# Products whose result is never read, in TensorE's queue during the first batch's attention

## The chip, the core and the metric

The kernel runs on one core of one Trainium2 chip. The metric is the device time of one execution in microseconds (us), as the median of several runs. Work is spread over five engines with a queue each: TensorE (PE, products and transposes), VectorE (DVE), ScalarE (ACT), GpSimd (POOL) and SyncE (SP), which here only issues transfers. Each engine takes the instructions of its queue in order; semaphores make one engine wait for another or for a transfer.

## What is computed

Three stages on 4 sequences of 576 positions, 512 wide, in float32:

```python
q_d, k_d, v_d = (t.reshape(B, H, Sd, 4, D).mean(axis=3) for t in (q, k, v))
out_d = sm_attn(q_d, k_d, v_d)                 # attention over 144 means
scores = np.where(abs(i - j) < 4, scale * q @ k.T, -1e9)
x = np.repeat(out_d, 4, axis=2) + softmax(scores) @ v

xk = mu_k * x + (1 - mu_k) * x_prev            # x_prev: the position before
xr = mu_r * x + (1 - mu_r) * x_prev
x = sigmoid(xr @ w_r) * (np.maximum(xk @ w_k, 0) ** 2 @ w_v)

h = np.maximum(x @ w_in, 0)
out = (h * sigmoid(conv3(h)) @ w_out)          # conv3: three taps along the sequence
```

There are 8 heads of 64, w_k and w_in are 512 x 1024, w_v and w_out 1024 x 512, w_r 512 x 512.

## The kernel before

The attention of a batch is done by groups of four heads (two groups, `gp` 0 and 1), and in the first batch each group also in two parts of the sequence: blocks 0 to `half`, then the rest. One part of one group is a chain of steps over four engines, each named by its tag:

- `ld`: SP loads kq (keys and queries), vw (the windows of v) and vp (v for the means). For the first batch, DVE folds vp to vd (L455, L456) and sums kq to kqd (L476, tag `kd`).
- `s`, local scores: PE adds the mask by products of `ident16` with `mask` (L504) and the scores (L513) in an a2 buffer of PSUM; DVE takes the maximum off (L530, L531), ACT the exponential (L539), DVE sums and normalizes (L542, L484, L485, L548) into probs.
- `ds`, down scores, over the means: PE (L575), DVE maximum (L591, L592), ACT exponential with sums (L598), DVE normalizes (L610) into pd.
- `do`: PE transposes pd (L639), ACT copies that to pdt (L647), PE multiplies by vd (L662), ACT copies to od (L674, L676).
- `lo`: PE transposes probs (L694), ACT copies to pt (L699), PE multiplies by vw (L713), DVE adds od and writes xT (L728).

Then `mix_prep` makes xk from xT: an ACT and a DVE instruction for each of four row blocks (L776, L782). The first half of the first batch goes through `first_mix` in plain float32: for each of eight column blocks `mt` of w_k an up product (L808, mm buffers of PSUM in turn: `mt` 0 in `mm_t[0]`, `mt` 1 in `mm_t[1]`), then relu and square on ACT (L820, L825) or DVE (L827), then the down products with w_v (L836). The second part of the first batch's attention and the first group of the second batch's are woven in between. All later halves go through `mix` (L869, L918) with each number split in two fp32r parts, three products in place of one; then gate, hidden layer and output (L1180, L1221, L1301).

A weight slice of 512 KB is loaded to one of three st_d buffers (L374), cut to a float on ACT and DVE (L379, L380, L361, L364) into one of four st_f buffers (st_f, st_ff), and split into its fp32r parts (L400 or L402, L406). An st_f buffer is free when the product that reads it and the split are done, an st_d buffer when L364 is.

The order isn't that of the code. Every piece of work is a `step` with an engine, an estimated time, the keys that it reads and writes, and at most a due time. `Program.order` computes for each step the latest time at which it should start, from its due time and from those that need it, less a number by tag from the table `EARLY`; then it plays the program through: an engine that is free takes, of the steps that are ready by its own estimates, that with the lowest latest time. That play sets each engine's order for good. A step that needs more estimated time therefore moves others, on all engines and to the end of the program.

Of the kernel before, what the change touches and what calls it, by code (L numbers as in the profile page):

```python
# [61 lines left out]
def windows(S, FAC):  # L62

    BQ = 32
    W = BQ + 2 * (FAC - 1)
    return BQ, W, [min(max(BQ * i - FAC + 1, 0), S - W) for i in range(S // BQ)]


class Program:
# [15 lines left out]
    def step(self, engine, us, f, r=(), w=(), due=None, slack=1.0):  # L85
        n = len(self.steps)
        deps = set()
        for k in r:
            if k in self.writer:
                deps.add(self.writer[k])  # L90
        for k in w:
            deps.update(self.readers.pop(k, ()))
            if k in self.writer:
                deps.add(self.writer[k])
        for k in r:
            self.readers.setdefault(k, set()).add(n)
        for k in w:
            self.writer[k] = n
        deps.discard(n)
        self.steps.append((engine, us, f, due, slack))  # L100
        self.tags.append(self.tag)
        self.deps.append(deps)
        return n
# [95 lines left out]
def dve(n):  # L199
    return 0.13 + 1.1e-3 * n  # L200
# [6 lines left out]
def act(n):  # L207
    return 0.155 + 0.93e-3 * n
# [6 lines left out]
def pe(n):  # L215
    return 6.6e-3 + 0.439e-3 * n
# [3 lines left out]
def tile_local_attention__then__channel_mix__then__conv_glu(  # L220
# [16 lines left out]
    nc = tc.nc  # L237
    B, NP, P, S = kq.shape
# [10 lines left out]
    BQ, W, starts = windows(S, FAC)  # L249
# [13 lines left out]
    prog = Program({"DVE": nc.vector, "POOL": nc.gpsimd, "ACT": nc.scalar})  # L263
    both = ("DVE", "POOL")
    step = prog.step
# [11 lines left out]
    ident16 = const.tile([P, P], BF16, name="ident16")  # L277
# [7 lines left out]
    mask = const.tile([P, 3, W], BF16, name="mask")  # L285
# [17 lines left out]
    def several(pool_, n, shape, dtype, name):  # L303
        return [pool_.tile(shape, dtype, name=f"{name}{i}") for i in range(n)]
# [14 lines left out]
    kqd = several(att, 1, [P, 2, 2 * SD], F32, "kqd") + several(first, 1, [P, 2, 2 * SD], F32, "kqd_f")  # L319
# [14 lines left out]
    mm_t = several(ps, 2, [P, 512], F32, "mm")  # L334
# [6 lines left out]
    def ring(name, tiles, one=0):  # L341

        i = count[name] = count.get(name, -1) + 1
        i %= one or len(tiles)
        return tiles[i], (name, i)
# [40 lines left out]
    def weight(src, hi, lo, r, nr, c0, key, need=(), use=None, c_at=0):  # L386

        prog.tag = key, r // nr, c0
        f, fk = floats(src, r, nr, c0)
        if use is not None:  # L390
            prog.tag = key, "first"
            use(f, fk)
            prog.tag = key, "parts", r // nr, c0
        nc_ = 512 // nr
        at = (slice(None), slice(r, r + nr), slice(c0 - c_at, c0 - c_at + nc_))
        part = (r // nr, c0 // nc_)

        def high(e):
            if e is nc.scalar:
                e.copy(hi()[at], f)  # L400
            else:
                e.tensor_copy(hi()[at], f)  # L402

        step(("ACT", "DVE"), (0.62, 0.43), high, [fk, *need], [(key, "h", *part)])
        step(
            "DVE", 0.69, lambda: nc.vector.tensor_sub(lo()[at], f, hi()[at].bitcast(F32)),  # L406
            [fk, (key, "h", *part), *need], [(key, "l", *part)],
        )
# [5 lines left out]
    def group(b, gp):  # L414
# [3 lines left out]
        g = {"kq": [ring("kq", kq_t, 2 * (b > 0)) for _ in pairs], "kqd": ring("kqd", kqd, int(b > 0)), "vw": ring("vw", vw_t, int(b > 0)),  # L418
             "vd": ring("vd", vd_t, int(b > 0))}
# [260 lines left out]
        def local_out(i0, i1):  # L680
# [24 lines left out]
            for pr, hp in enumerate(pairs):  # L705
# [30 lines left out]
                step("DVE", 0.8, add, [odk], [(pk, 0), (pk, 1)] + ks, slack=SL[i0 > 0])  # L736

        return {"loads": loads, "kqd": pooled_kq, "s": local_scores, "ds": down_scores,
                "do": down_out, "lo": local_out}

    def store_x(b):
        prog.tag = "sx", b
# [9 lines left out]
    PACE = 1.32  # L752

    def due(us, pace=1.0):
        t = clock[0]
        clock[0] += us * pace
        return t

    def mix_prep(b, nh):
        prog.tag = "mp", b, nh  # L760
        c0 = nh * NH
        whole = b == nh == 0
        if not whole:
            xk, key = ring("xk", xk_t)
        fs = []
        for kt in range(KM):
            x = xT[b % 2][:, kt]
            cur, prev = x[:, 1 + c0:1 + c0 + NH], x[:, c0:c0 + NH]
            i = count["t"] = count.get("t", -1) + 1
            t, tk = tmp[:, i % 2], ("tmp", i % 2)  # L770
            n = (2, 3, 6, 7)[kt] if whole else 2 + i % 2
            f, fk = tmp[:, n], ("tmp", n)
            xs = [("xT", b % 2, kt, 0)] + ([("xT", b % 2, kt, half)] if nh else [])
            step(
                "ACT", 0.53,
                lambda t=t, prev=prev, kt=kt: nc.scalar.activation(  # L776
                    t, prev, AF.Copy, scale=mus[:, 1, kt:kt + 1]),
                xs + ["mus"], [tk],
            )
            step(  # L780
                "DVE", dve(NH),
                lambda t=t, f=f, cur=cur, kt=kt: nc.vector.scalar_tensor_tensor(  # L782
                    out=f, in0=cur, scalar=mus[:, 0, kt:kt + 1], in1=t, op0=ALU.mult, op1=ALU.add),
                xs + [tk], [fk],
            )
            if whole:
                fs.append((f, fk))
                continue
            h, lo = xk[:, 0, kt], xk[:, 1, kt]
            step("ACT", act(NH), lambda h=h, f=f: nc.scalar.copy(h, f), [fk], [(key, 0, kt)])  # L790
            step(
                ("DVE",), (dve(NH),), lambda e, h=h, lo=lo, f=f: e.tensor_sub(lo, f, h.bitcast(F32)),
                [fk, (key, 0, kt)], [(key, 1, kt)],
            )
        return (fs,) if whole else (xk, key)

    def first_mix(xs):

        squares = xT[1].rearrange("p a s -> p (a s)")[:, 0:KF * NH].rearrange("p (k s) -> p k s", k=KF)
        over = [("xT", 1, x, c) for x in range(KM) for c in (0, half)]  # L800

        for mt in range(KF):
            pst, pk = ring("mm", mm_t)

            def up(w, wk, mt=mt, pst=pst, pk=pk):
                def f():
                    for kt in range(KM):
                        nc.tensor.matmul(  # L808
                            pst[:, 0:NH], lhsT=w[:, kt], rhs=xs[kt][0], start=(kt == 0), stop=(kt == KM - 1)
                        )  # L810

                us = 4 * KM * pe(NH)
                step("PE", us, f, [wk] + [k for _, k in xs], [pk], due=due(us, PACE))

            weight(w_k, lambda: wk_t[0], lambda: wk_t[1], 0, 4, mt * P, "wk", use=up)
            prog.tag = "up", 0, 0
            r, rk = tmp[:, 4 + mt % 2], ("tmp", 4 + mt % 2)
            step(
                "ACT", act(NH) - 0.03,
                lambda r=r, pst=pst: nc.scalar.activation(r, pst[:, 0:NH], AF.Relu), (), [pk, rk],  # L820
            )

            def square(e, r=r, mt=mt):
                if e is nc.scalar:
                    e.activation(squares[:, mt], r, AF.Square)  # L825
                else:
                    e.tensor_tensor(out=squares[:, mt], in0=r, in1=r, op=ALU.mult)  # L827

            step(("ACT", "DVE"), (act(NH), 0.46), square, [rk], [("sq", mt)])
        for mt in range(KM):  # L830
            pst, pk = ring("mm", mm_t)
            for a in range(0, KF, 4):
                def down(w, wk, a=a, pst=pst, pk=pk):
                    def f():
                        for kt in range(a, a + 4):
                            nc.tensor.matmul(  # L836
                                pst[:, 0:NH], lhsT=w[:, kt - a], rhs=squares[:, kt],
                                start=(kt == 0), stop=(kt == KF - 1),
                            )

                    us = 16 * pe(NH)
                    step(
                        "PE", us, f, [wk] + [("sq", kt) for kt in range(a, a + 4)] + over, [pk], due=due(us, PACE)
                    )

                weight(w_v, lambda: wv_t[0], lambda: wv_t[1], a, 4, mt * P, "wv", use=down)
            prog.tag = "dn", 0, 0
            out_of_mix(mt, pst, pk, 0)
# [93 lines left out]
    g0 = [group(0, gp) for gp in range(NG)]  # L942
# [16 lines left out]
    def attend(gs, i0, i1, later=None):  # L959
        for g in gs:  # L960
            g["kqd"](i0, i1)
            g["s"](i0, i1)
            g["ds"](i0, i1)
        for g in gs:
            g["do"](i0, i1)
            g["lo"](i0, i1)

    attend(g0, 0, half)
    xk = mix_prep(0, 0)
    for gp in range(NG):  # L970
        g0[gp]["loads"](half, NB)
# [432 lines left out]
```

## Time and profile before

| | |
|---|---|
| median of 3 runs | 584.84 us |
| lowest and highest run | 584.05, 585.73 us |
| span of the profiled execution | 584.2 us |
| PE busy | 553.3 us (95%), 5900 products |
| DVE, ACT, POOL busy | 380.5, 329.3, 52.0 us |
| chain of work that ended last | PE 82%, DVE 7%, DMA 5%, ACT 3% |

The span is that of the execution from its first to its last instruction; all times of the trace count from its start. "Idle before" is the time for which an engine stood still ahead of an instruction, and the name behind the arrow what ended it. The granted clock (PEclk) is a share of 2.4 GHz: 1.00 is that level, 0.50 is 1.2 GHz. An instruction's duration on PE reaches to a modelled end, so that those of a row overlap; where the time per instruction matters, it is read from start to start.

### The profile page before, as it was taken

How to read it: one execution, taken by the hardware profiler on the slowest of the kernel's cores; microseconds unless marked ns; L12 is line 12 of the kernel's file. 1: busy time of each engine (PE TensorE's matmuls, PEld its weight loads, DVE VectorE, ACT ScalarE, POOL GpSimd, SP SyncE). 2: the span in 40 equal slices, each digit the busy share in tenths (PEclk: the TensorE clock that was granted, in tenths of full speed). 3: DMA queues.
4: the chain of work that ended last, by engine and by line, in shares of the span. 5: the costliest groups of instructions: out<-in, count | busy, mean ns of one | idle time of the engine just before them, and what ended most of it. 6: DMA issues, size and time to landing. Idle time of an engine off the chain costs nothing.

```text
span 584.2 us, 14308 instructions
## 1 busy us (share of the span) xinstructions
PE 553.3 (95%) x5900; PEld 510.7 (87%) x5900; DVE 380.5 (65%) x795; ACT 329.3 (56%) x779; POOL 52.0 (9%) x133
## 2 busy tenths in 40 slices
PE   4579979899999999999999999999999999999996
PEld 3457758789999999999999999899899898998995
DVE  6787698688534355344925899587586686395580
ACT  2458678576646475455838865455454455363441
POOL 3002021021121312110000000000000000000000
PEclk9999989898999999999999999999999999999999
DMA  9858998869467576712530530310400400100101
GB/s 262 292 191 216 296 293 209 283 181 302 141 136 207 113 220 160 171 51 76 187 116 2 202 110 0 123 42 0 146 18 1 145 19 1 54 2 1 54 2 54
DMA packets 42449, 74.14 MB, mean 127 GB/s; under 512 B 3648, under 2 KB 28736, under 8 KB 41472
## 3 DMA queue, kind: packets, MB, share of 16 engines
q1 hardware_dynamic: 38064, 65.27, 33.7%
q0 software_dynamic: 4320, 7.97, 8.9%
q8 instruction: 46, 0.75, 0.5%
q14 instruction: 19, 0.16, 0.1%
HBM read 59.06 MB, written 14.16 MB: 125 GB/s over the span
## 4 chain that ended last, share of the span: by engine, by line
PE 82%; DVE 7%; DMA 5%; ACT 3%; issue 2%; SPq 1%; ACTq 0%; POOL 0%; DVEq 0%
PE a L1301 17%; PE mm L869 15%; PE mm L918 15%; PE a L1221 8%; PE mm L1221 7%; PE mm L1180 4%; PE a L1180 4%; PE a L713 3%; DMA st_d<-in_moe_w_k 2%; DMA st_d<-in_moe_w_v 2%; PE a L694 2%; PE mm L836 2%; PE mm L808 1%; PE a L513 1%; PE a L639 1%
## 5 line engine op out<-in xcount | busy, mean ns | idle before, releaser
L1301 PE MATMUL a<-wk,wv 128*128 128x512 f32 x432 | 100.9, 390 | 0.0
L918 PE MATMUL mm<-k,wv 128*128 128x288 f32 x672 | 97.4, 301 | 0.2 <-ACT tmp L888 0.2
L1301 PEld LDWEIGHTS a<-wk,wv 128*128 128x128 f32 x432 | 80.9, 188 | 15.8
L869 PE MATMUL mm<-xk,wk 128*128 128x288 f32 x672 | 94.6, 299 | 0.0
L918 PEld LDWEIGHTS mm<-k,wv 128*128 128x128 f32 x672 | 91.9, 191 | 0.8 <-ACT tmp L888 0.5
L869 PEld LDWEIGHTS mm<-xk,wk 128*128 128x128 f32 x672 | 91.1, 191 | 1.1 <-issue 0.5
L1221 PE MATMUL mm<-k,wi 128*128 128x386 f32 x288 | 53.2, 338 | 0.4 <-ACT k L1205 0.3
L1221 PE MATMUL a<-k,wi 128*128 128x386 f32 x288 | 53.1, 338 | 0.0
L906 DVE TENSOR_TENSOR k<-tmp,k 128x288 fp32r<-128x288 f32 x56 | 25.7, 464 | 41.9 <-ACT k L899 41.2
L1221 PEld LDWEIGHTS mm<-k,wi 128*128 128x128 f32 x288 | 50.7, 188 | 1.5 <-ACT k L1205 0.7
L1221 PEld LDWEIGHTS a<-k,wi 128*128 128x128 f32 x288 | 50.8, 188 | 0.2
L728 DVE TENSOR_TENSOR xT<-a,od 128x288 f32<-128x288 f32 (+2 forms) x40 | 13.8, 392 | 37.6 <-PE a L713 37.6
L1276 ACT ACTIVATE tmp<-tmp 128x384 f32<-128x384 f32 x48 | 25.1, 523 | 21.6 <-DVE tmp L1270 21.6
L1266 DVE TENSOR_SCALAR tmp<-h,cw_sb 128x384 f32<-128x384 f32 x48 | 20.0, 417 | 25.6 <-ACT h L1251 12.2
L888 ACT ACTIVATE tmp<-mm 128x288 f32<-128x288 f32 x56 | 23.0, 412 | 22.3 <-PE mm L869 22.1
L1270 DVE SCALAR_TENSOR_TENSOR tmp<-h,cw_sb,tmp 128x384 f32<-128x384 f32 x48 | 29.7, 619 | 2.6
L1267 DVE SCALAR_TENSOR_TENSOR tmp<-h,cw_sb,tmp 128x384 f32<-128x384 f32 x48 | 29.7, 619 | 2.3
L1316 ACT ACTIVATE xT<-a 128x512 f32<-128x512 f32 x18 | 10.3, 597 | 36.2 <-PE a L1301 34.4
L1286 ACT CAST wv<-tmp 128x384 fp32r<-128x384 f32 x48 | 24.1, 511 | 9.3 <-DVE tmp L1279 9.2
L1279 DVE SCALAR_TENSOR_TENSOR tmp<-tmp,h 128x384 f32<-128x384 f32 x48 | 25.9, 553 | 3.0 <-ACT tmp L1276 2.5
L1288 DVE TENSOR_TENSOR wv<-tmp,wv 128x384 fp32r<-128x384 f32 x48 | 25.7, 553 | 2.9 <-ACT wv L1286 2.3
L361 DVE SCALAR_TENSOR_TENSOR st_f<-st_f,st_d 128x512 uint32<-128x512 uint32 x28 | 20.3, 725 | 11.1 <-ACT st_d L380 10.8
(149 smaller groups left out, 889.1 us busy)
## 6 DMA issues: line engine op xcount, KB each, us to landing
kq<-in_kq SPq DMA_DIRECT2D x12, 576.0 KB, 5.0
vw<-in_vw SPq DMA_DIRECT2D x6, 1152.0 KB, 9.5
kqd<-in_kqp POOLq DMA_DIRECT2D x18, 288.0 KB, 5.5
x_d<-xT SPq DMA_DIRECT2D x16, 288.0 KB, 7.0
v_d<-tmp SPq DMA_DIRECT2D x32, 144.0 KB, 4.0
out_dram<-xT SPq DMA_DIRECT2D x18, 256.0 KB, 2.0
st_d<-in_moe_w_k SPq DMA_DIRECT2D x8, 512.0 KB, 4.5
st_d<-in_moe_w_v SPq DMA_DIRECT2D x8, 512.0 KB, 5.4
```

Source lines behind the costliest of these rows:

```text
L869: nc.tensor.matmul(pst[:, 0:NH], lhsT=wk_t[wt][:, kt, mt * P:(mt + 1) * P], rhs=xk[:, xs, kt, :], start=(kt == 0 and g == 0), stop=(kt == ...
L906: ("DVE",), (dve(NH),), lambda e, r=r, kh=kh, kl=kl: e.tensor_sub(kl, r, kh.bitcast(F32)),
L918: nc.tensor.matmul(pst[:, 0:NH], lhsT=wv_t[wt][:, kt, mt * P:(mt + 1) * P], rhs=xs, start=(kt == 0 and g == 0), stop=(kt == KF - 1 and g = ...
L1180: nc.tensor.matmul(pst[:, 0:CW], lhsT=late["wr"][wt][:, kt, mt * P:(mt + 1) * P], rhs=r_t[xs][:, kt, :], start=(kt == 0 and g == 0), stop= ...
L1221: nc.tensor.matmul(pst[:, 0:CW], lhsT=late["wi%d" % (mt * P // HF)][wt][:, kt, mt * P % HF:mt * P % HF + P], rhs=x1s[xs][:, kt, :], start= ...
L1267: nc.vector.scalar_tensor_tensor(out=cv, in0=tap(0), scalar=cw[:, 0, mt:mt + 1], in1=cv, op0=ALU.mult, op1=ALU.add)
L1270: nc.vector.scalar_tensor_tensor(out=cv, in0=tap(2), scalar=cw[:, 2, mt:mt + 1], in1=cv, op0=ALU.mult, op1=ALU.add)
L1276: step("ACT", act(CH), lambda: nc.scalar.activation(cv, cv, AF.Tanh, scale=0.5), (), [cvk])
L1279: lambda: nc.vector.scalar_tensor_tensor(out=gt, in0=cv, scalar=1.0, in1=tap(1), op0=ALU.add, op1=ALU.mult),
L1286: step("ACT", act(CH), lambda: nc.scalar.copy(gh, gf), ["wv_old", gk], [("gh", j)])
L1288: ("DVE",), (0.56,), lambda e: e.tensor_sub(gl, gf, gh.bitcast(F32)),
L1301: nc.tensor.matmul(pst, lhsT=xs[:, tt * P:(tt + 1) * P], rhs=wo[wt][:, kt, :], start=(kt == 0 and g == 0), stop=(kt == KF - 1 and g == 2),)
```

## The change

56 steps of a new tag, `fill`, are recorded behind the first part of the first batch's attention. Each is two products of the bf16 identity with one row of the mask, spread to 8 x 38 = 304 columns, into `mm_t[1]`. A step is estimated at 0.4 us; it needs one half of the first group's kqd and is due at 1e5, that is, never by itself. The second up product (`mt` 1), which overwrites `mm_t[1]`, now also needs all 56, so that each fill gets its latest time from that product. Nothing reads what the fills write.

```diff
-        return {"loads": loads, "kqd": pooled_kq, ..., "lo": local_out}
+        return {"loads": loads, "kqd": pooled_kq, ..., "lo": local_out, "kqd_key": g["kqd"][1]}
...
                 us = 4 * KM * pe(NH)
-                step("PE", us, f, [wk] + [k for _, k in xs], [pk], due=due(us, PACE))
+                step(
+                    "PE", us, f, [wk] + [k for _, k in xs] + (fills if mt == 1 else []), [pk], due=due(us, PACE)
+                )
...
     attend(g0, 0, half)
+    prog.tag = "fill",
+    fills = [("fill", i) for i in range(56)]
+    for k in fills:
+        def fill():
+            for _ in range(2):
+                nc.tensor.matmul(
+                    mm_t[1][:, 0:8 * W], lhsT=ident16, rhs=mask[:, 1:2, :].to_broadcast([P, 8, W]),
+                    start=True, stop=True,
+                )
+
+        step("PE", 0.4, fill, [(g0[0]["kqd_key"], 0, 1)], [k], due=1e5)
     xk = mix_prep(0, 0)
```

On PE, the end of the second group's first part stood like this before (`a` are PSUM buffers, the numbers tell them apart; the next product with `mm` is the first up product):

```order
L694 MATMUL a_159<-ident,probs_f_140 128x128
L713 MATMUL a_161<-pt_141,vw_f_136 64x32 x20
L713 MATMUL a_160<-pt_141,vw_f_136 64x32 x20
L575 MATMUL a_161<-kqd_133 32x144 x8
L504 LDWEIGHTS ident_71
L504 MATMUL a_160<-mask,ident_71 128x152
```

The same place now; where lines are left out stand further pairs of the fill:

```order
L694 MATMUL a_159<-ident,probs_f_140 128x128
L976 LDWEIGHTS ident_71
L976 MATMUL mm_157<-mask,ident_71 128x304
...
L713 MATMUL a_161<-pt_141,vw_f_136 64x32 x20
L976 LDWEIGHTS ident_71
L976 MATMUL mm_157<-mask,ident_71 128x304
...
L575 MATMUL a_161<-kqd_133 32x144 x8
L976 LDWEIGHTS ident_71
L976 MATMUL mm_157<-mask,ident_71 128x304
...
L713 MATMUL a_160<-pt_141,vw_f_136 64x32 x20
L639 MATMUL a_158<-ident,pd_142 72x128 x4
L575 MATMUL a_161<-kqd_f_134 32x144 x8
```

Six pairs stand ahead of the first L713, six behind it and twelve behind L575, which now comes ahead of the second L713; the scores (L504) of the next part come later. From the first scores on, the runs of pairs ahead of these are 16 (ahead of the second group's scores), 2 (within them), 16 (ahead of L639), 10 (ahead of L662), 24 (ahead of L694), 6 (ahead of the first group's L713), 10 (ahead of the second group's L662) and 4 (ahead of its last L694).

On DVE, during the scores of the second group's first part, as a piece of the difference:

```order
 L476 TENSOR_REDUCE kqd_f_134<-kq_f_132 128x224
 L610 TENSOR_TENSOR pd_142<-pd_142,sums_148 128x432
+L455 TENSOR_TENSOR xT_120<-xT_120 72x1024
+L456 TENSOR_TENSOR vd_137<-xT_120 72x512
 L530 TENSOR_REDUCE sums_149<-a_160 128x5
 L531 TENSOR_TENSOR probs_f_140<-a_160,sums_149 128x5x38
```

The fold of the first group's vd, which stood behind the second group's down scores, now stands ahead of its local scores.

## Rows read from the trace of the kernel before

**Rows 1.** Windows of PE: stretch, length, busy (instructions), granted clock, DMA share, GB/s
```profile
0.00:40.00 40.00, 22.90 (x559) 1.00 0.79 244
7.83:36.00 28.17, 16.91 (x354) 1.00 0.79 235
40.00:66.00 26.00, 26.00 (x383) 1.00 0.90 250
66.00:141.00 75.00, 66.84 (x1106) 0.93 0.86 253
141.00:584.00 443.00, 437.58 (x3893) 1.00 0.30 88
```

**Rows 2.** Timeline of PE, first attention: start, us, instructions, idle before, releaser
```profile
19.95 2.23 PE L662 MATMUL a<-pdt,vd 72*64 72x64 f32 x32 [4.71 <-DVE vd L456]
...
30.45 1.92 PE L662 MATMUL a<-pdt,vd_f 72*64 72x64 f32 x32 [0.88 <-ACT pdt L647]
...
33.59 2.40 PE L713 MATMUL a<-pt,vw_f 38*64 38x32 f32 x80
```

**Rows 3.** Timeline of PE, equal up and equal down products of the first mix
```profile
40.04 4.21 PE L808 MATMUL mm<-tmp,st_f 128*128 128x288 f32 x8
...
45.16 2.21 PE L808 MATMUL mm<-tmp,st_f 128*128 128x288 f32 x8
...
82.41 3.54 PE L836 MATMUL mm<-xT,st_f 128*128 128x288 f32 x8
...
87.65 2.11 PE L836 MATMUL mm<-xT,st_f 128*128 128x288 f32 x8
```

**Rows 4.** Windows of PE in two of these products
```profile
40.00:42.00 2.00, 2.00 (x12) 1.00 0.77 244
82.00:84.00 2.00, 2.00 (x7) 0.50 0.99 273
```

**Rows 5.** The page: granted clock in 40 equal slices of 14.6 us
```profile
PEclk9999989898999999999999999999999999999999
```

**Rows 6.** Timeline of PE behind 44 us, steps like those of the first part
```profile
47.30 1.12 PE L662 MATMUL a<-pdt,vd 72*64 72x32 f32 x32
...
60.32 1.13 PE L713 MATMUL a<-pt,vw_f 38*64 38x32 f32 x64
...
65.78 0.91 PE L513 MATMUL a<-kq 64*32 64x38 f32 x80
...
112.28 0.96 PE L575 MATMUL a<-kqd 64*32 64x144 f32 x40
...
120.11 1.25 PE L639 MATMUL a<-ident,pd 128*72 128x128 f32 x10
```

**Rows 7.** Mask products near 65 us by narrow windows, and all weight loads of L504
```profile
65.40 0.46 PE L504 MATMUL a<-mask,ident 128*128 128x304 bf16 x3
65.53 0.32 PE L504 MATMUL a<-mask,ident 128*128 128x304 bf16 x2
L504 PEld LDWEIGHTS <-ident x36: 95/98/152, 3.9 to 256.4; 128*128 128x128 bf16 x36
```

**Rows 8.** Timelines of DVE (three rows) and ACT (the last), first attention
```profile
16.11 0.69 DVE L361 SCALAR_TENSOR_TENSOR st_f<-st_f,st_d 128x512 uint32<-128x512 uint32 x1 [1.52 <-ACT st_d L380]
...
17.89 1.19 DVE L455 TENSOR_TENSOR xT<-xT 72x1024 f32<-72x1024 f32 x1
...
22.43 0.55 DVE L548 TENSOR_TENSOR probs<-probs,sums 128x380 f32<-128x380 f32 x1
...
17.46 0.79 ACT L647 COPY pdt<-a 72x768 f32<-72x768 f32 x1
```

**Rows 9.** Waits of PE from 66 to 141 us: total, times, longest
```profile
PE a L513 <- issue: 2.4, 1, 2.4
PE a L639 <- DVE probs L531: 1.8, 1, 1.8
PE mm L836 <- DVE st_ff L364: 1.3, 2, 0.8
```

More of the change, by code (lines that the diff above doesn't have):

```diff
@@ L738, in group @@
         return {"loads": loads, "kqd": pooled_kq, "s": local_scores, "ds": down_scores,
-                "do": down_out, "lo": local_out}
+                "do": down_out, "lo": local_out, "kqd_key": g["kqd"][1]}
     def store_x(b):
```

## The prediction

> **What bounds the kernel now.** I read the busy time by stage first [rows 1]. Behind 141 us TensorE (PE) stands still for 5.4 of 443 us, so whatever moves the end must happen ahead of that: any us by which PE is through with the early work sooner or later is a us of the end. Between 40 and 66 us PE has no gap. Up to 40 us it is busy 22.9 of 40 us, and between 66 and 141 us it loses 8.2 us in waits. Next came PE's timeline from 7.8 to 36 us: small steps of the first batch's attention, each released by VectorE (DVE) or ScalarE (ACT) of the step before it, with waits like the 4.71 us at 19.95 [rows 2]; PE works 16.9 of these 28.2 us and stands still for 11.3. Third, the level of PE's clock [rows 3, 4]. Eight instructions of the first up product took 4.21 us from 40.04 on and the next eight, of the same shape, 2.21 us, behind a stretch in which PE had not stood still from 40 us on. The same doubling stands at 82.41 (3.54 us against 2.11 for equal work), and there the granted clock reads 0.50, the 1.2 GHz level. At 40 us the column reads 1.00, so in this early stretch it can't be trusted, and I go by durations: the attention steps ahead of 40 us also take longer than equal ones behind it [rows 2, 6]: L713 (80 instructions) 2.40 us against 1.13 for 64, L662 1.92 against 1.12. So the kernel spends its first 44 us at 1.2 GHz, and the first batch's steps are on the path to L808, the first up product.
>
> **What the change costs.** It adds 56 steps of two products each, 112 pairs of a weight load (128x128 bf16) and a 304-column bf16 product. They wait for nothing but a DVE sum that the first down scores need too, and no other engine works for them. All stand ahead of the second up product: 88 pairs between the first group's scores and the last L694, and 24 behind that, around the first L713 of the second group, L575 and the second L713, which the order shows. Their price is in the trace [rows 7]: among the mask products at 65.4 us one 304-column product starts at 65.40 and the next at 65.53, though a weight load of 98 ns belongs to each; that is 0.13 us per pair at 2.4 GHz, and I take twice that, 0.26 us, at 1.2 GHz (the ratio of 4.21 to 2.21). The first 16 stand in a row from about 7.6 us on. I take 13 pairs at the low level (3.4 us, a little less than the first up product stayed at it [rows 3]) and 99 at the high one: 3.4 + 12.9 = 16.3 us.
>
> [...]
>
> **What it gives back.** If the fills hold PE's clock up from about 11 us on, PE's own steps shrink. Before, from 7.8 (end of the first scores) to 36.0 (end of the last L713) PE works 16.9 us [rows 1]. At the high level the same steps come to 8.7 us by [rows 6], less about 0.1 to 0.25 us for the tail of each step's last instruction, which what stands behind now hides: scores and down scores 1.5 (80 L513 0.7, 24 of 40 L575 0.55, masks 0.25), two L639 (six of ten) 1.3, two L662 2.1, ten L694 (like L639) 1.15, two L713 (80 where the row has 64) 2.65. With L575 pulled ahead of the last L713 it is 9.2.
>
> Not every gap can be filled, because the order was planned with 0.2 us for each product: where it lines up fewer than the real wait takes, PE still waits. DVE and ACT move little. DVE's fold of v (L455 and L456, the first alone 1.19 us [rows 8]) now stands ahead of the second group's scores, into the 1.52 us in which DVE waited for ACT ahead of L361; behind it the scores and thereby ACT's L598 and L647 come about 0.4 us later, and the last L548 of the group ends at 23.7 and not 22.98, because a second fold stands ahead of it. So PE waits for pdt (L647, about 18.6 in place of 18.25, with PE there at 17.15: 1.5 us), for L548 (0.9), and some 1.1 in small pieces: 3.5 us. Sum: 7.6 + 16.3 + 9.2 + 3.5 = 36.6 us for the end of the last L713, against 36.0 before. The fills don't make the attention end sooner; they pay for themselves, and a little over.
>
> **The lead behind it.** In what follows nothing was added. Before, 11.3 us pass from there to the end of the second up product (the start of L662 at 47.30 [rows 3, 6]). At the high level the same rows give 8.4 us: L639 0.5, L575 0.45, scores 0.85, L662 1.05, up 2.1, L639 0.5, scores 0.6, up 2.1, and 0.3 of waiting for the mixed x. So the second up product ends at 45.0, 2.3 us sooner, and one L662 and one L639 (1.6 us), which before came behind it, are done. PE leads by 3.9 us.
>
> **What is late next.** The up and down weights come through three st_d buffers that SP refills when DVE has cut the slice before; each cut waits for a PE product to free its st_f. So the loads lead with PE. SP's queue is changed too: vd is loaded ahead of two kq, and a w_v slice ahead of two stores of x; both change the order alone. But DMA is 0.86 to 0.90 busy from 40 to 141 us [rows 1], and the two places where PE waits for L364, the cut, cost 1.3 us now [rows 9]. A PE that arrives sooner waits longer there: between nothing and the whole lead. I take that these waits double, 1.35 us, since the loads hang on PE and shift with it for the most part. Lead kept: 3.9 - 1.35 = 2.5 us. The profiled execution spans 584.2 us, 0.6 below the median of 584.84 us; the change is the same for both, so 584.84 - 2.5 = **582.3 us**.
>
> **Rivals.** *The lead is given back.* PE's waits between 66 and 141 us (L639 for L531 1.8, L364 1.3, L513 2.4 [rows 9]) are for chains of DVE, ACT and DMA that don't get faster; with all of 3.9 us given back the time is 584.8, the same. For it speaks the DMA share, against it that each cut is released by a product. *The weight load is not hidden.* If a pair takes 0.228 us at the high level, the fills take 25.5 us and not 14.6; step by step the run of 24 behind L662, which could end 0.9 us ahead of its wait, now ends 2.3 us behind it, and from there on everything that is added is late: the last L713 ends at 42.1, 5.5 us later, and with it xT, the mixed x and all up products: 587.8 us, slower. It decides from about 0.16 us a pair on; the pitch in [rows 7] speaks against it, but it rests on two products. [...] *Another order later.* The planner's order differs all the way down, since each start time moved; PE's waits between 66 and 141 us and the three drops of the clock in that stretch (three 8s in [rows 5], the first of them 0.50 at 82 us and 1.4 us dearer by [rows 3]) may come out otherwise: 2 us of gain or 4 of loss, 580 to 587 us. *The clock doesn't rise.* If the fills run at 1.2 GHz throughout, 112 x 0.26 = 29.1 us meet 11.3 us of gaps, and the end is 18 us later, 603 us; against it speaks that without a break PE rose at 44 us.
>
> **How the numbers follow.** About 0.3% (1.75 us) is what a measurement of this kernel can tell from no change. The forecast has 0.46; the lead given back 0.27; the unhidden weight load 0.11; an unlucky order 0.12; no rise of the clock 0.04. Of what is faster, the most is the whole lead and one spared drop: 584.84 - 3.9 - 1.4 = 579.5. The range reaches from there to the unhidden load at 587.8. Faster 0.46, same 0.27, slower 0.27.
>
> **What would show it.** Right: L976 products 0.13 us apart from about 11 us on; L713 of the first batch at about 1.4 us for 80; the last L713 at 36 to 37 us; the first up product's eight instructions in 2.1 to 2.3 us; the second up product over by 45 us; PE full from there to 66 us; waits for L364 of 2 to 3 us. Wrong: fills 0.2 us or more apart, L713 of the second group behind 40 us, or the eight instructions still at 4 us; or, with all of that right, gaps between 66 and 141 us of 12 us in place of 8.

## The result and the profile after

The change made the kernel slower: 591.78 us (median of 7 runs, 586.81 to 593.06) against 585.73 us for the kernel before on the same chip (7 runs, 583.74 to 589.76), a ratio of 1.012 with a 95% interval of 1.0085 to 1.0155. The forecast was 582.3 us, with a range to 587.8. The profiled execution of the changed kernel spans 589.3 us, 5.1 us more than that of before. In its lines L836, L869 and L918 of before are L838, L871 and L920, the relu L820 is L822, and the added products are L976.

The first part went nearly as forecast. TensorE's (PE's) timeline answers to [rows 2, 3]:

```profile
7.73 3.17 PE L976 MATMUL mm<-mask,ident 128*128 128x304 bf16 x16
...
14.24 0.45 PE L575 MATMUL a<-kqd_f 64*32 64x144 f32 x9 [1.49 <-issue]
14.63 2.36 PE L976 MATMUL mm<-mask,ident 128*128 128x304 bf16 x16
...
20.26 3.45 PE L976 MATMUL mm<-mask,ident 128*128 128x304 bf16 x24
...
26.73 1.37 PE L713 MATMUL a<-pt,vw 38*64 38x32 f32 x80 [1.15 <-ACT pt L699]
...
37.91 0.79 PE L713 MATMUL a<-pt,vw_f 38*64 38x32 f32 x40
...
41.86 2.21 PE L808 MATMUL mm<-tmp,st_f 128*128 128x288 f32 x8
...
44.88 2.21 PE L808 MATMUL mm<-tmp,st_f 128*128 128x288 f32 x8
46.92 0.60 PE L694 MATMUL a<-ident,probs 128*128 128x128 f32 x4
```

The first 16 fills take 3.17 us, the next 16 take 2.36, and 24 in a row 3.45 (0.14 to 0.15 us each, with the tail of the last). Up to 9.5 us the fills start 0.25 us apart, which is 1.20 columns a ns and the low level, the prediction's 1.2 GHz; from there on they start 0.14 us apart. So the rise to the high level, its 2.4 GHz, at which equal products start 0.24 us apart in place of 0.48 (L838 below), came within the first run of fills, the 80 products of L713 take 1.37 us in place of 2.36 to 2.40, and the first up product 2.21 in place of 4.21. The second up product starts at 44.88 and the row behind it at 46.92, where before that point came at 47.30.

Between 61 and 97 us the lead goes. PE's timeline of that stretch in the changed kernel (the fourth row stands for the first products of the second batch's attention with v, the last for the next stage):

```profile
60.44 1.14 PE L713 MATMUL a<-pt,vw_f 38*64 38x32 f32 x64
63.93 3.90 PE L838 MATMUL mm<-xT,st_f 128*128 128x288 f32 x8 [2.35 <-ACT tmp L822]
...
86.58 0.66 PE L694 MATMUL a<-ident,probs 128*128 128x128 f32 x4 [3.16 <-ACT pdt L647]
...
94.64 2.30 PE L713 MATMUL a<-pt,vw 38*64 38x32 f32 x144
96.87 1.33 PE L871 MATMUL mm<-xk,wk 128*128 128x288 f32 x8
```

The same two points of the kernel before:

```profile
94.11 2.30 PE L713 MATMUL a<-pt,vw 38*64 38x32 f32 x144
96.34 1.86 PE L869 MATMUL mm<-xk,wk 128*128 128x288 f32 x12
```

At 60 us the changed kernel had done one up product of 2 us more than before; at 94 it is 0.5 us behind. ScalarE's (ACT's) timeline tells what PE waited for at 63.93 and 86.58:

```profile
62.38 0.66 ACT L379 ACTIVATE st_f<-st_d 128x512 f32<-128x512 f32 x1 [3.00 <-DMA st_d<-in_moe_w_v]
62.94 0.64 ACT L380 ACTIVATE st_d<-st_d 128x512 uint32<-128x512 uint32 x1
63.48 0.40 ACT L822 ACTIVATE tmp<-mm 128x288 f32<-128x288 f32 x1
...
85.07 0.66 ACT L379 ACTIVATE st_ff<-st_d 128x512 f32<-128x512 f32 x1 [2.27 <-DMA st_d<-in_moe_w_v]
85.63 0.64 ACT L380 ACTIVATE st_d<-st_d 128x512 uint32<-128x512 uint32 x1
86.17 0.35 ACT L647 COPY pdt<-a 72x256 f32<-72x256 f32 x1
```

The relu L822 had its product long before, and so had the copy L647; both stood in ACT's queue behind a conversion (L379, L380) that waited for a slice of w_v. At the first of the two places the kernel before has such a wait too, and a longer one; PE worked its last two up products meanwhile and then waited 0.36 us. In the new order the eighth up product stands behind the first down product (at 67.66) and covers nothing:

```profile
61.38 4.15 PE L808 MATMUL mm<-tmp,st_ff 128*128 128x288 f32 x16
65.47 0.67 ACT L379 ACTIVATE st_f<-st_d 128x512 f32<-128x512 f32 x1 [3.63 <-DMA st_d<-in_moe_w_v]
```

Behind both of these waits of PE, and behind a pause of 2.14 us at 141, the granted clock fell (windows of 2 us; the columns are stretch, length, busy time of PE, PEld, DVE, ACT and POOL with their instructions, granted clock, DMA share, GB/s):

```profile
64.20:66.20 2.00, 2.00 (x5) 1.40 (x5) 1.97 (x7) 0.77 (x2) 0.00 (x0) 0.50 1.02 316
89.20:91.20 2.00, 2.00 (x6) 1.43 (x5) 1.97 (x5) 1.94 (x6) 0.00 (x0) 0.50 0.90 291
142.80:144.80 2.00, 2.00 (x10) 2.00 (x9) 1.53 (x4) 0.42 (x2) 0.00 (x0) 0.50 0.98 348
```

Each is the low level. The eight products from 63.93 take 3.90 us where equal ones take 2.1 (they start 0.48 us apart, the others 0.24). Before also had three such drops, at 82, 106 and 133 us, so their number is no difference between these two traces, and standing still doesn't settle it by itself: behind a pause of 2.54 us that ends at 106.38 the clock reads 1.00 up to 141 us (the window from 106.37 below). Over all executions there is a difference. The median of their mean granted clocks is 0.985 for the changed kernel (7 executions) and 0.986 in its second measurement (12), against 0.993 for the kernel before on the chip of the second (35); 0.007 of 585 us is 4 us of PE's work (an estimate, 2 us by the means). No other version lies under 0.988. What holds the clock lower there isn't shown.

Behind 97 us the lag grows from 0.5 to 5 us. A part is order again: PE's products stand otherwise between 120 and 130 us, many steps of ACT and DVE too, and PE waits 1.14 us for DVE's xT at 137.63, for which it didn't wait before. What stands out on PE's timeline are pauses that end in "issue":

```profile
106.38 0.30 PE L513 MATMUL a<-kq 64*32 64x38 f32 x16 [2.54 <-issue]
...
137.63 0.48 PE L504 MATMUL a<-mask,ident 128*128 128x38 bf16 x4 [1.14 <-DVE xT L728]
138.04 1.07 PE L513 MATMUL a<-kq 64*32 64x38 f32 x101
141.25 0.59 PE L513 MATMUL a<-kq 64*32 64x38 f32 x43 [2.14 <-issue]
...
208.67 1.49 PE L920 MATMUL mm<-k,wv 128*128 128x288 f32 x10 [0.49 <-issue]
...
217.06 2.15 PE L871 MATMUL mm<-xk,wk 128*128 128x288 f32 x15 [1.04 <-issue]
```

With the one at 14.24 they sum to 7.7 us; before had two, 2.39 us at 105.5 and 0.50 at 132.4. The one at 141 cuts a row of 144 equal products, for which nothing was missing, in two. Where do they stand? Windows from one resumption to the next, first of the changed kernel, then of before, count the products and the weight loads between them (PE, then PEld):

```profile
106.37:141.24 34.87, 30.38 (x512) 28.35 (x511) 28.91 (x56) 24.08 (x58) 7.06 (x7) 1.00 0.82 226
141.24:208.66 67.42, 66.49 (x1023) 64.11 (x1024) 30.84 (x74) 35.63 (x96) 12.47 (x13) 0.97 0.57 158
208.66:217.05 8.39, 7.35 (x128) 6.93 (x128) 4.93 (x11) 4.51 (x12) 0.90 (x1) 1.00 0.93 246
```

```profile
105.49:132.43 26.94, 25.32 (x384) 23.82 (x383) 21.69 (x43) 18.86 (x47) 4.93 (x5) 0.94 0.74 213
```

To within a record these are 1024, 2048, 256 and 768 instructions, each a multiple of 256. These two traces have seven such pauses; with every instruction of PE counted from the start, those on semaphores among them, all seven stand 193 past a multiple of 256. The transfers of 138.5 to 141.5 us hold one packet of the queue for instructions, and those of 134 to 138.5 and of 141.5 to 144 none:

```profile
q8 instruction: 1, 0.02, 1.9%
```

The whole execution has 47 of these packets, of 16 KB each, for 12024 products and weight loads, that of before 46 for 11800: one to 256. Each of the seven pauses, 193 past k times 256, ended 1.2 to 1.6 us behind the end of the k-th packet, and no edge of the two traces was passed sooner behind its packet. So PE's instructions arrive in blocks of 256, and at these edges PE stood still until the next one was there. The change adds 224 instructions to PE's queue, and with that other work stands behind each later edge. What an edge costs is another matter: in the second measurement of the same kernel (after_again below) the same row ran uncut:

```profile
139.09 1.45 PE L513 MATMUL a<-kq 64*32 64x38 f32 x144
```

### The profile page after: what moved, and what is told of

It reads as the page before. It is cut to its first block, busy times and chain, and to the rows that moved or that the text cites. A ratio compares the mean times of both kernels' runs of the same rounds, so it can differ in the third digit from the quotient of the medians.

```text
span 589.3 us, 14520 instructions
## 1 busy us (share of the span) xinstructions
PE 561.0 (95%) x6012; PEld 513.6 (87%) x6012; DVE 381.7 (65%) x799; ACT 327.7 (56%) x775; POOL 52.5 (9%) x133
## 4 chain that ended last, share of the span: by engine, by line
PE 76%; DMA 10%; DVE 7%; ACT 3%; issue 2%; SPq 0%; ACTq 0%; POOL 0%
PE a L1314 17%; PE mm L871 14%; PE mm L920 13%; PE a L1234 8%; PE mm L1234 7%; PE a L1193 4%; PE mm L1193 4%; DMA st_d<-in_moe_w_v 3%; DMA vw_f<-in_vw 2%; PE a L713 2%; DMA st_d<-in_moe_w_in 2%; PE mm L838 2%; PE a L513 1%; DMA kq_f<-in_kq 1%; PE a L662 1%
## 5 line engine op out<-in xcount | busy, mean ns | idle before, releaser
L920 PE MATMUL mm<-k,wv 128*128 128x288 f32 x672 | 95.9, 298 | 1.0 <-issue 0.5
L871 PE MATMUL mm<-xk,wk 128*128 128x288 f32 x672 | 95.1, 300 | 1.3 <-issue 1.0
L871 PEld LDWEIGHTS mm<-xk,wk 128*128 128x128 f32 x672 | 91.2, 191 | 2.9 <-issue 1.6
L920 PEld LDWEIGHTS mm<-k,wv 128*128 128x128 f32 x672 | 90.4, 188 | 1.8 <-issue 0.8
L908 DVE TENSOR_TENSOR k<-tmp,k 128x288 fp32r<-128x288 f32 x56 | 27.1, 485 | 42.1 <-ACT k L901 41.4
L379 ACT ACTIVATE st_f<-st_d 128x512 f32<-128x512 f32 x28 | 18.9, 675 | 17.3 <-DMA st_d<-in_moe_w_k 8.9
```

Source lines behind the costliest of these rows:

```text
L871: nc.tensor.matmul(pst[:, 0:NH], lhsT=wk_t[wt][:, kt, mt * P:(mt + 1) * P], rhs=xk[:, xs, kt, :], start=(kt == 0 and g == 0), stop=(kt == ...
L908: ("DVE",), (dve(NH),), lambda e, r=r, kh=kh, kl=kl: e.tensor_sub(kl, r, kh.bitcast(F32)),
L920: nc.tensor.matmul(pst[:, 0:NH], lhsT=wv_t[wt][:, kt, mt * P:(mt + 1) * P], rhs=xs, start=(kt == 0 and g == 0), stop=(kt == KF - 1 and g = ...
```

## The experiments

Three theories were put against each other. **Order**: the planner's new order, of PE and of ACT, costs the time. **Blocks**: the shifted block edges cost it. **Slices**: the transfers of w_v set the pace from 63 to 94 us, so that a lead of PE is worth nothing. All ratios are to the kernel before on the same chip, with 95% intervals; the groups of runs stood on different chips, so versions of different groups are compared by their ratios.

### Order, fills and edges taken apart

order_alone keeps the changed kernel's order and emits no fills:

```diff
-            for _ in range(2):
+            for _ in range(0):
                 nc.tensor.matmul(mm_t[1][:, 0:8 * W], lhsT=ident16, ...
```

> The order of the changed kernel on every engine, with the 56 steps planned but no product issued for them (so TensorE is at 1.2 GHz up to its first long run of work, as before). Theory 'order': the loss comes from the order that the planner made for a TensorE that is late, so the time is that of the changed kernel or more, 589 to 593 us, with its waits of some 2 to 3 us for ACT between 60 and 90 us. Theory 'blocks': the loss comes from 224 more TensorE instructions, which move the edges of the 16 KB blocks in which instructions are fetched, so that other short products stand behind an edge; here none is added, so the time is near that of the kernel before, 584 to 587 us, with at most one or two issue waits, 3 us together.

Measured: 590.51 us, ratio 1.0059 (1.0027 to 1.0092), as theory "order" had it. The new order alone, in a PE that stays at the low level as before (the first up product takes 3.98 us from 47.55 on), is slower than the old one: PE now waits in places that the fills were to cover, and the second up product starts 7.5 us later than with them. So this is not the price of the order with the fills in it:

```profile
PE a L639 <- DVE probs_f L531: 3.8, 1, 3.8
PE a L504 <- DVE probs L531: 3.4, 1, 3.4
...
52.34 2.21 PE L808 MATMUL mm<-tmp,st_f 128*128 128x288 f32 x8
```

old_order_112 is the other half: the order of before on every engine, and 112 pairs of fills in PE's queue alone, ahead of named steps.

```diff
+FILLS = {(('s', 0, 1, 0), 0): 16, (('s', 0, 1, 0), 1): 2, (('do', 0, 0, 0), 0): 16, ...}
 ...
+            if engine == "PE":
+                self.between(k, n)   # FILLS[k, n] pairs ahead of the n-th PE step with this tag
```

> The order of the kernel before on every engine, with the 112 pairs of the fill put into TensorE's queue alone, in runs like those of the changed kernel. Theory 'order': without the new order the lead is kept, 581 to 583 us. Theory 'blocks': the block edges lie as in the changed kernel, so issue waits of 4 us and more come behind 100 us, 586 to 590 us. Theory 'slices': whatever the order, the last down products of the first half wait for weight slices that the transfers bring no sooner, so L713 of the second batch's first group starts at about 94 us as before, and the time is 584 to 587 us.

Measured: 587.0 us, ratio 1.0008 (0.9973 to 1.0044). The same work in the old order costs nothing measurable, and brings nothing either; the 581 to 583 us of theory "order" are missed, and both others hold 587.

old_order_realigned adds 16 one-column pairs, so that 256 instructions are added in all and the edges behind them stand as in before; after_realigned does the same to the changed kernel.

```diff
+TINY = {(('lo', 0, 0, 0), 2): 16}
 ...
+            nc.tensor.matmul(mm_t[1][0:1, 0:1], lhsT=ident16[:, 0:1], rhs=mask[:, 1, 0:1], ...)
```

> As old_order_112 with 16 more pairs of one column and one weight column, so that 256 instructions (16 KB) are added and the block edges behind them lie as in the kernel before. Theory 'blocks': 2 to 5 us less than old_order_112, 583 to 585 us, and issue waits behind 100 us only where the kernel before has them (2.4 and 0.5 us). Theory 'order': like old_order_112, within 1.5 us.

> The changed kernel with 16 more pairs of one column, ahead of the first L713 where TensorE waits 1.1 us anyway, so that the block edges behind them lie as in the kernel before. Theory 'blocks': 2 to 5 us less than the changed kernel, 586 to 589 us, without the issue waits at 208 and 217 us. Theory 'order': no less than the changed kernel, 590 to 592 us.

Measured: 584.42 us, ratio 0.9982 (0.9942 to 1.0022), and 586.4 us, ratio 1.0015 (0.9977 to 1.0054). The second is the clearer: more products, and yet 0.6 to 1.0% less than the changed kernel (1.012, and 1.0078 when measured again below). The two differ in the order alone, on one chip and with equal fills and equal counts of instructions: the new order is 0.3% behind the old one, with intervals that overlap.

### The edges alone, and other numbers of instructions

tiny_only puts one-column pairs where old_order_112 has its fills: the same 224 instructions, next to no work, and no earlier rise of the clock.

> The kernel of before, its order kept on every engine, with 112 one-column products (a one-column weight each) at the places where old_order_112 had its fills: they add the same 224 instructions to TensorE's queue, but next to no busy time, so the clock rises no sooner than in before (44 us). Theory 'blocks' (what slows the changed kernel is that 224 more instructions put other work behind the edges of the 256-instruction blocks that TensorE fetches): pauses that end in 'issue' sum to 5 to 7 us in place of 2.9, and the time is 2 to 4 us above before, ratio 1.004 to 1.007. Theory 'order' (the new order alone slows): no more than 1 us above before, ratio 0.998 to 1.002, since no order is changed.

Measured: 588.31 us, ratio 1.0044 (1.0016 to 1.0072), with pauses of 2.92 and 2.07 us behind 38 us:

```profile
107.49 0.38 PE L535 MATMUL a<-kq 64*32 64x38 f32 x15 [2.92 <-issue]
...
139.09 1.59 PE L940 MATMUL mm<-k,wv 128*128 128x288 f32 x10 [2.07 <-issue]
```

This is the purest of the runs: no order is changed, the first up product still takes 4.21 us, as in before, and the kernel is slower. By the starts of equal products its trace is 0.9 us behind at 66 us (what the pairs themselves cost at most), and 3.0 from 141 us on.

old_order_92 drops 20 of the 112 pairs, so that 184 instructions are added; old_order_92_and_60 adds 60 one-column pairs to that, 304 in all. By a count of short blocks in the trace of before the first should meet the fewest pauses and the second the most.

> The kernel of before with 92 of the fill pairs in the same gaps (20 dropped from the later gaps), its order kept on every engine: 184 more instructions on TensorE. By the trace of before, counted in blocks of 256, a shift of 184 leaves the fewest blocks that are short in time. Theory 'blocks': pauses that end in 'issue' of under 3 us in the whole run, the early clock kept (rise at 8 to 11 us), and 3 to 5 us below before, ratio 0.992 to 0.995. If the pauses were nothing and the fills all: 2 us below before as old_order_realigned, ratio 0.997. If fills bring nothing in this order: ratio 1.000.

> The same 92 fill pairs with 60 one-column products beside them in the same gaps: 304 more instructions, a shift that by the trace of before puts the most short blocks behind an edge. Theory 'blocks': pauses of 6 us or more, and 3 to 5 us slower than old_order_92, ratio to before 0.999 to 1.004. If the pauses do not matter: as old_order_92, within 1 us.

Measured: 582.21 us, ratio 0.9964 (0.9932 to 0.9996), and 582.17 us, ratio 0.9954 (0.9926 to 0.9982). The first came near what was expected of it, the second missed outright: it is no slower than the first. The pauses behind 38 us sum to 2.0 and 4.1 us, so the shift did move them, but by less than my count said. Which edge costs how much can't be read from the trace of a kernel whose edges stand elsewhere.

PE's timeline of old_order_92 shows what the fills are worth where the order stays:

```profile
41.01 2.21 PE L830 MATMUL mm<-tmp,st_f 128*128 128x288 f32 x8
43.14 1.13 PE L684 MATMUL a<-pdt,vd 72*64 72x32 f32 x32
...
91.08 2.30 PE L735 MATMUL a<-pt,vw 38*64 38x32 f32 x144
```

The second up product ends 4.2 us ahead of before (43.14 against 47.30), and 3.0 of them are left at the second batch's products with v (91.08 against 94.11).

after_again is the changed kernel beside these three.

> The changed kernel again, beside these on one chip. Theories 'order' and 'blocks' both: 4 to 7 us above before, ratio 1.007 to 1.012, with pauses of 6 to 8 us. If its first measurement was a matter of the chip: within 2 us of before.

Measured: 589.85 us, ratio 1.0078 (1.0048 to 1.0108). The loss stands, a little smaller. The pauses were missed: the profiled execution has 3.3 us of them (1.2 at 15 us, 1.6 at 108, 0.5 at 213) and not 6 to 8, and at 586.7 us it is one of the shortest of the twelve. Against the first trace, that is 4.4 us of pauses and 4.4 us of time less, with the same instructions in the same order (other waits and the clock differ a little too).

### What ACT's queue and the slices take

after_cuts_later leaves PE's queue alone and moves the two conversions on ACT behind the relu and the copy that stood behind them; after_cuts_later_realigned has the 16 one-column pairs as well.

```diff
+        o = self.order()
+        for cut, behind in ((210, 193), (246, 385)):   # step numbers: L379 behind L822, L379 behind L647
+            o.remove(cut)
+            o.insert(o.index(behind) + 1, cut)
```

> The changed kernel with two steps moved on ACT alone: the conversion of a slice that stood waiting 3.0 us for its transfer ahead of the relu of the seventh up product (62.4 us) now stands right behind that relu, and the one that waited 2.3 us ahead of the second copy into pdt (85.1 us) right behind that copy. TensorE's queue and all others are untouched. Theory 'order' (the lead is given back because ACT, which works its queue in order, stands still ahead of work that TensorE waits for): the first down product's wait of 2.4 to 3.8 us falls under 0.7, the wait for pdt of 3.2 under 1, the second batch's first products with v start 2 to 3 us sooner than in the changed kernel (near 92 in place of 94.6), and the time falls by 2 to 4 us, ratio to before 1.001 to 1.006. Theory 'slices' (the transfers of w_v set the pace from 63 to 94 us whatever stands ahead): the waits only move to the conversions' results (L364), those products still start at 94 to 95, and the ratio stays at 1.007 to 1.012.

> The same two moves, with 16 one-column product pairs ahead of the first product with v as in after_realigned, so that 256 instructions are added in all and the 256-instruction blocks begin where they did in before. Theory 'order': 2 to 4 us under after_realigned, ratio to before 0.995 to 0.999. Theory 'slices': as after_realigned, ratio 1.000 to 1.003.

Measured: 586.62 us, ratio 1.0033 (1.0000 to 1.0066), and 583.36 us, ratio 0.9990 (0.9957 to 1.0024). The times came out as theory "order" had them, and in the version with the 16 pairs as well the loss against before is gone. Of the waits, the one for the relu is gone and that for pdt fell from 3.9 to 0.7 us in all, but 1.1 us came back as a wait for a slice and 1.6 as one for pt, whose copy now stands behind the second conversion (waits of after_cuts_later; its L698 is L694):

```profile
PE a L698 <- ACT pt L703: 1.6, 1, 1.6
PE mm L842 <- DVE st_ff L368: 1.1, 1, 1.1
...
PE a L698 <- ACT pdt L651: 0.7, 1, 0.7
```

In its profile the second batch's products with v start at 94.85 us, no sooner than in the changed kernel, since that execution was already 2.35 us later at 40 us; from there it gained 2.1 us. In the realigned one they start at 90.06, against 92.60 in after_realigned, though it was 1.3 us later at 41 us.

after_short_v and before_short_v ask what the slices hold. Both load an eighth of the second batch's first tile of v and leave the rest out, so 1.0 MB less stands ahead of the slices.

```diff
+            ez = (e1 - e0) // 8 if (b, gp) == (1, 0) else e1 - e0
 ...
-                t[:, e0:e1].rearrange(...), vw[b, gp, :, e0 * 4 * D:e1 * 4 * D],
+                t[:, e0:e0 + ez].rearrange(...), vw[b, gp, :, e0 * 4 * D:(e0 + ez) * 4 * D],
```

> The changed kernel, with the second batch's first transfer of v cut to an eighth of its columns (the rest of that tile keeps the first batch's numbers), so that 1.0 MB less stands among the transfers ahead of the slices of w_v. Theory 'slices': the slices land some 3 us sooner, the conversions' waits of 3.0 and 2.3 us nearly go, the second batch's first products with v start at 90 to 92, and the time is 3 to 4 us under the changed kernel, ratio to before 1.001 to 1.006. If the transfers are not what those conversions wait for in the end (a buffer that comes free late instead): no change, ratio 1.007 to 1.012.

> The kernel of before with the same transfer cut to an eighth. Theory 'slices' (both kernels are paced by w_v's transfers from 63 to 94 us): it gains as much as the changed kernel does, 2 to 4 us, ratio 0.993 to 0.997. Theory 'order' (in before's order little waits for the slices: 1.3 us in all): it gains 1 us at most, ratio 0.998 to 1.000.

Measured: 583.53 us, ratio 1.0004 (0.9971 to 1.0037), and 583.49 us, ratio 0.9961 (0.9932 to 0.9990). Both gain, the changed kernel 0.7 to 1.2% and before 0.4%, so what is loaded there paces both. PE's timelines, after_short_v first:

```profile
62.06 2.21 PE L839 MATMUL mm<-xT,st_f 128*128 128x288 f32 x8 [0.31 <-ACT tmp L823]
...
82.65 0.66 PE L695 MATMUL a<-ident,probs 128*128 128x128 f32 x4 [2.77 <-ACT pdt L648]
...
90.72 2.30 PE L714 MATMUL a<-pt,vw 38*64 38x32 f32 x144
```

```profile
90.64 2.30 PE L714 MATMUL a<-pt,vw 38*64 38x32 f32 x144
```

With less ahead of the slices the first wait of 2.35 us is 0.31, while the second stays at 2.77, and both kernels reach the products with v at the same time: the early lead is lost in the new order even then. ACT's conversion ahead of the second wait still stands 1.97 us for its slice.

### The later edges

after_late_16 puts the 16 one-column pairs into the changed kernel at 131 us, so that only edges behind that place move.

```diff
+                    if (b, nh, mt, a) == (0, 1, KM - 1, 0):
+                        for _ in range(16):
+                            nc.tensor.matmul(pst[0:1, 0:1], lhsT=ident16[:, 0:1], rhs=mask[:, 1, 0:1], ...)
```

> The changed kernel with 16 one-column product pairs at 131 us, ahead of the last tile's first down product of the first batch's second mix: the first 130 us stay as in the changed kernel, and behind that place the 256-instruction blocks begin where they did in before. Theory 'blocks late' (much of the loss stands behind 130 us, at the pauses of 2.1, 0.5 and 1.0 us at 141, 209 and 217 us): those three pauses sum to under 1.2 us in place of 3.6, and the time falls by 2 to 4 us, ratio to before 1.002 to 1.006. Rival (what made the realigned kernels faster was something that the 16 pairs did at 25 us, or the early edges): ratio 1.007 to 1.012, as the changed kernel.

Measured: 589.08 us, ratio 1.0037 (1.0008 to 1.0066). The ratio lies in the range of "blocks late", but its interval reaches that of the changed kernel (from 1.0048), and the pauses came out only in part as expected. Those at 209 and 217 us are gone (in after_again the one at 209 was so without any change). The one at 141 is not:

```profile
142.13 0.94 PE L513 MATMUL a<-kq 64*32 64x38 f32 x85
145.19 0.72 PE L513 MATMUL a<-kq 64*32 64x38 f32 x59 [2.11 <-issue]
```

It cuts the same row of 144 products, behind 85 of them where the changed kernel has 101: 16 pairs were added, and the edge stands 16 products sooner. That ties the place of these pauses to a count of instructions, and to nothing that the products themselves do. The rival, that the 16 pairs at 25 us did something else for the realigned versions, is not out.

## Why the prediction was wrong

- **The price of the fills and the level of the clock: right.** 0.14 to 0.15 us a pair at the high level, tail included, and the rise in the first run, at 9.5 us, were forecast at 0.13 and about 11 us. The rival of the unhidden weight load (0.228 us a pair) and that of a clock that stays low are out.
- **The sum up to 40 us: 2 us short.** The last L713 ends at 38.7 and not 36.6. The waits are not what it lacked: from 7.6 us on PE is busy for 27.6 of 31.1 us, so it stands still for 3.5 us, the forecast figure. That is luck, for the members are others: 1.49 us of a pause at 14.24 and 1.15 for L699 at 26.73, with 0.4 for pdt and 0.3 for L548 where 1.5 and 0.9 were forecast. Too small were the two terms of work: by the starts of instructions the fills take 17.5 us and not 16.3, about 0.1 us more at each end of a run, and PE's own steps 10.1 and not 9.2.
- **The lead: half.** The second up product ends at 46.92 and not 45.0, which is that shortfall; the lead was 2 us and not 3.9.
- **What is late next: the step that failed.** I put the slices at PE's own waits for L364 and doubled them. In the changed kernel PE doesn't wait for L364 at all; the slices hold ACT, and behind ACT's conversions stand a relu and a copy that PE needs at once (waits of 2.35 and 3.16 us). So nothing of the lead is left at 94 us, where the sum kept 2.5 us. The sum had looked at the queues of PE, DVE and SP, and at ACT's only for its start times. Moving these two conversions won back 0.4 to 0.9%, by the two measurements of the changed kernel, and 0.25% in the realigned pair, whose intervals overlap.
- **The rival of the lead given back.** In this stretch it is what happened, and transfers are what ACT waits for. They don't take the lead by themselves: old_order_92 keeps 3.0 of 4.2 us at the same place.
- **The rival of another order.** It held 0.12 and ended at 587 us. In part it is what happened, by more than its price: order_alone, without fills, is 0.6% slower than before, while 92 of the pairs in the old order are 0.4% faster and all 112 no different from before. Gaps between 66 and 141 us were to rise to 12 us; they are 9.9 (75 less 65.06 busy) against 8.2. The greater part of the lag comes behind 97 us, much of it behind 141, where [rows 1] had made me look for nothing.
- **What no step of it had: the block edges.** The wait of L513 for "issue" stood in [rows 9], and I read it as a wait for a chain that doesn't get faster. It was such a pause. The sum puts the shift of the edges at nothing; tiny_only gives its price in the old order, 0.44%, of which the pairs themselves may be up to 0.9 us. In the new order realigning won 0.6 to 1.0%, and 0.4% with the conversions moved, where the intervals overlap.

What single runs give against before: 92 fill pairs in the old order -0.4%, the new order without fills +0.6%, 224 nearly empty instructions +0.4%; in the changed kernel 32 more instructions take 0.6 to 1.0% away, the two moves on ACT 0.4 to 0.9%, both together all of the loss. These are not parts of one sum, as each is taken in another kernel. Open stays how much each single edge costs: the late edges alone gave a ratio between those of the changed and the realigned kernel, and 304 more instructions cost nothing beside 184. Open stays also how much of the loss is the lower granted clock. The runs of one kernel spread over 5 to 11 us, about as much as the whole loss or more, so a single trace can't divide it further.

A version faster than both kernels came out on the way: old_order_92, 0.36% under before (0.04 to 0.68%), and old_order_92_and_60 with 0.46% (0.18 to 0.74%), which can't be told from it.

## What to carry to other kernels

Filling gaps to hold the clock up paid here only where 92 pairs were put into a finished order (0.4%; 112 brought nothing measurable). Given to the planner as steps of 0.4 us they moved every later start, and with two steps of ACT moved and 32 instructions added the kernel was only as fast as before again. When a lead is to be carried on, read the queue of every engine that PE waits for, and look for instructions that stand there ahead of PE's and wait for a transfer. And count instructions: when a change adds some hundred of them to an engine that has no gaps left, look for idle time that ends in "issue", and measure the same kernel with a few empty instructions more.

## What the runs showed of the hardware

PE's pauses stand at multiples of 256 instructions, counted between them (1024, 2048, 256 and 768), and cost up to 3.4 us (waits of after_cuts_later_realigned). The one at 141 us ended 1.5 us behind a packet of the instruction queue, which has 47 packets in 0.77 MB, 16 KB each. The cost belongs to the execution and not to the program alone: at the same edge of the same row it was 2.14 us in the changed kernel's trace and nothing in that of after_again. The pauses fell where many short products stand in a row, as L513 (101 of 144 products in 1.07 us), and at some edges behind longer ones; at most edges there is none (five pauses beside 47 packets in the changed kernel's trace). They were 7.7 us of that execution, of which 6.2 behind 40 us, where PE stands still for 20 us in all.
